# First MoE chunk: weights asked for in pairs; wide copies of probabilities moved to VectorE in the sink-free groups

## The chip, the cores and the metric

The kernel runs on one core of one Trainium2 chip. The metric is the device time of one execution in microseconds (us), median of several runs. The engines are TensorE (PE; its weight loads are PEld), VectorE (DVE), ScalarE (ACT), GpSimd (POOL) and SyncE (SP), which issues most DMAs. Each engine takes its own instructions in the order of the program and waits where one isn't ready.

## The reference

Attention with sink keys and a sliding window, then two feed-forward layers:

```python
# attention: q, k, v are 2 x 8 heads x 768 x 64, n_sink = 4, window = 128
scores = scale * q @ k.T
keep = is_sink | in_window
scores = np.where(keep, scores, -1000000000.0)
a = np.exp(scores - max); a = a / (sum(a) + 1e-09)
x = (a @ v)                      # as 1536 tokens x 512
# MoE 1: 512 -> 1536 -> 512
g = x @ w_gate; silu = g * (1.0 / (1.0 + np.exp(-g)))
x = silu * (x @ w_val) @ w_out
# MoE 2: 512 -> 2048 -> 512
h = x @ w_in
g = np.maximum(h, 0.0) + alpha * np.minimum(h, 0.0)
out = g @ w_out
```

The expert weights arrive as 64-bit floats (the kernel reads them as pairs of 32-bit words) and are split on the chip.

## The kernel before, in words

**Attention.** Tokens are handled in 24 groups: two heads (one head pair, `hp`) by two query blocks of 128. The first eight, numbered 0 to 7 here in program order, begin at query block 0 of a sequence (`i0 == 0`) and are sink-free: their keys are only blocks 0 and 1. `attention()` runs a software pipeline over groups: scores of group x, values of group x-2, flips of group x-1, `norm` of x, `prep` of x+2.

- `prep` transposes k and q on PE and copies them out on ACT (`th`).
- `scores` (L265) makes two score tiles for each of the two query blocks t = 0, 1. DVE adds the mask and takes a row maximum (L271; in later groups after a predicated copy, L269); ACT takes the exponential and its row sum (L275, `pr`).
- `norm` makes reciprocals of the sums on DVE (L291, L292, `rinv`); POOL multiplies the probabilities by them (L298 in sink-free groups, L307 and L308 in others).
- `flip` transposes probabilities on PE (L320, `ps_p` in PSUM) and copies them to SBUF as `pt`. In sink-free groups ACT does this (L324), 256 columns wide for t = 0 and 512 for t = 1. In the others DVE multiplies by a triangle mask on the way (L326, 512 wide).
- `values` multiplies by v on PE (L351, `xp`); ACT rounds the result to `xh` (L847), DVE makes the rest `xl` (L848).

**Weights.** `Stream` loads weight tiles of 128x512 in the order of `seq` (SP), and `convert` turns each into a rounded part `wh` and a rest `wl`: ACT (L587), DVE TENSOR_SCALAR (L589), DVE SCALAR_TENSOR_TENSOR twice (L592, L595), ACT `wh` (L604), DVE `wl` (L605). One tile is converted at each call of `tick`, into one of 12 slots; seven more slots are added when attention is over. `done` gives slots back. `moe1_seq` writes the order of the first layer: chunks of four gate tiles (`wg`), four value tiles (`wv`), four output tiles (`wo`).

**MoE.** `Moe1.unit(c, b)` handles chunk c of the hidden features for 512 tokens (pass b): for each pair of features two gate products `pg`, then two value products `pv`, each 12 matmuls (L656 to L658: `wh` by `xh`, `wh` by `xl`, `wl` by `xh`, for four slices kk of the 512 inputs, one for each head pair), then the output product `po`. Pass 0 needs `xh` and `xl` of groups 0 to 7; slice kk needs the two groups of head pair kk, the last of them groups 4 to 7. Units (0, 0) and (0, 1) are woven between attention groups 8 to 23; the last pass of chunk 0 and all else run after attention.

The order on each engine is decided by the framework's scheduler when the program is built; an edit at one place can so move instructions of others.

Of the kernel before, what the change touches and what calls it, by code (L numbers as in the profile page):

```python
# [11 lines left out]
AF = mybir.ActivationFunctionType  # L12
# [11 lines left out]
NF1 = FF1 // P  # L24
# [9 lines left out]
CHUNK = 4  # L34
# [10 lines left out]
DOWN = float(2.0**-112)  # L45
# [94 lines left out]
class Group:  # L140
# [169 lines left out]
    def flip(self, t):  # L310
        nc, g = self.nc, self.g
        w, blk, sp, kk = self.blocks(t)
        if t == 0:
            self.pt = g.pt_p.tile([P, 2, 2 * NG, P], F32, tag="pt", name="pt")
        nb = len(blk)
        ps = g.ps_t.tile([P, 512], F32, tag="ps", name="ps_p")
        for e in range(2):
            for x, c in enumerate(blk):
                y = (e * nb + x) * P
                nc.tensor.transpose(ps[:, y:y + P], self.pr(t, e, c, P), g.ident)  # L320
        b0 = max(0, 2 * t - self.off)
        psv = ps[:, :2 * nb * P].rearrange("p (e c) -> p e c", e=2)
        if sp is None:
            nc.scalar.activation(self.pt[:, :, b0:b0 + nb].rearrange("p e a c -> p e (a c)"), psv, AF.Copy)  # L324
        else:
            nc.vector.tensor_tensor(  # L326
                out=self.pt[:, :, b0:b0 + 2], in0=psv.unsqueeze(2).to_broadcast([P, 2, 2, P]),
                in1=g.tri.unsqueeze(1).to_broadcast([P, 2, 2, P]), op=ALU.mult,
            )
        if t == NG - 1 and self.sink:  # L330
            self.pts = g.pt_p.tile([P, P], F32, tag="pts", name="pts")
            ps = g.ps_t.tile([P, 512], F32, tag="ps", name="ps_p2")
            nc.tensor.transpose(ps[:, 0:P], self.sk.rearrange("p x s -> p (x s)"), g.ident)
            nc.scalar.activation(self.pts, ps[:, 0:P], AF.Copy)
# [203 lines left out]
def new_acc(g, name):  # L538
    for pool in g.acc_ps:
        if pool[1]:  # L540
            pool[1] -= 1
            return pool[0].tile([P, KD, T], F32, tag="acc", name=name), pool
    assert False


def big(g, dt, name):
    return g.x_p.tile([P, KD, T], dt, tag="x", name=name)
# [83 lines left out]
def moe1_seq(wg, wv, wo):  # L631
    seq = []
    for c in range(NF1 // CHUNK):
        fs = range(c * CHUNK, (c + 1) * CHUNK)
        step = CHUNK if c == 0 else 2
        for f in fs[::step]:
            seq += [(0, wg, x, DOWN, x) for x in range(f, f + step)]
            seq += [(0, wv, x, DOWN, NF1 + x) for x in range(f, f + step)]
        seq += [(1, wo, f, DOWN, 2 * NF1 + f) for f in fs]
    return seq  # L640

# [10 lines left out]
def proj(nc, ps, w, xh, xl):  # L652
    wh, wl = w
    for kk in range(KD):
        c = slice(kk * P, (kk + 1) * P)
        nc.tensor.matmul(ps, wh[:, c], xh[:, kk], start=(kk == 0), stop=False)  # L656
        nc.tensor.matmul(ps, wh[:, c], xl[:, kk], start=False, stop=False)  # L657
        nc.tensor.matmul(ps, wl[:, c], xh[:, kk], start=False, stop=(kk == KD - 1))  # L658
# [5 lines left out]
def hidden_pair(g):  # L664
    return [g.h_p.tile([P, 2, T], F32R, tag=t, name=t) for t in ("hh", "hl")]


def split_hidden(nc, hid, hh, hl):
    nc.scalar.activation(hh, hid, AF.Copy)  # L669
    nc.vector.tensor_tensor(out=hl, in0=hid, in1=hh, op=ALU.subtract)  # L670


class Moe1:
# [4 lines left out]
    def unit(self, c, b):  # L678
        nc, g, st = self.nc, self.g, self.st
        nch = NF1 // CHUNK  # L680
        w0 = self.base + c * 3 * CHUNK

        def at(kind, x):
            return w0 + (kind * CHUNK + x if c == 0 else 2 * (x - x % 2) + 2 * kind + x % 2)

        xh, xl = self.xs[b]
        last = b == len(self.xs) - 1
        hid_of = []
        for x in range(0, CHUNK, 2):
            pair = hidden_pair(g)  # L690
            pss, sgs = [], []
            for r in range(2):
                ps = g.ps_m.tile([P, 512], F32, tag="ps", name="pg")
                proj(nc, ps, st.get(at(0, x + r)), xh, xl)
                pss.append(ps)
                if r == 0:
                    yield
            for ps in pss:
                sg = g.t_p.tile([P, T], F32, tag="sg", name="sg")
                nc.scalar.activation(sg, ps, AF.Silu)  # L700
                sgs.append(sg)
            yield
            for r in range(2):
                hh, hl = (t[:, r] for t in pair)
                ps = g.ps_m.tile([P, 512], F32, tag="ps", name="pv")
                proj(nc, ps, st.get(at(1, x + r)), xh, xl)
                hid = g.t_p.tile([P, T], F32, tag="hid", name="hid")
                nc.vector.tensor_tensor(out=hid, in0=ps, in1=sgs[r], op=ALU.mult)  # L708
                split_hidden(nc, hid, hh, hl)
                hid_of.append((hh, hl))  # L710
                if last and r == 1 and (c or x + 2 == CHUNK):
                    st.done(4 if c else 2 * CHUNK)
                yield
        if c == 0:
            self.accs[b] = new_acc(g, "acc1")
        acc, home = self.accs[b]
        if c == nch - 1:
            yh, yl = big(g, F32R, "yh"), big(g, F32R, "yl")
        for m in range(KD):
            mc = slice(m * P, (m + 1) * P)  # L720
            ps = g.ps_m.tile([P, 512], F32, tag="ps", name="po")
            for x, (hh, hl) in enumerate(hid_of):
                wh, wl = st.get(w0 + 2 * CHUNK + x)
                nc.tensor.matmul(ps, wh[:, mc], hh, start=(x == 0), stop=False)  # L724
                nc.tensor.matmul(ps, wl[:, mc], hh, start=False, stop=False)  # L725
                nc.tensor.matmul(ps, wh[:, mc], hl, start=False, stop=(x == CHUNK - 1))  # L726
            av = acc[:, m]
            if c == 0:
                nc.scalar.activation(av, ps, AF.Copy)
            else:  # L730
                nc.vector.tensor_tensor(out=av, in0=ps, in1=av, op=ALU.add)
            if c == nch - 1:
                split_hidden(nc, av, yh[:, m], yl[:, m])
            yield
        if c == nch - 1:
            home[1] += 1
            self.put(yh, yl)
        if last:
            st.done(CHUNK)
# [78 lines left out]
def fast(nc, tc, ctx, g, n_sink, window, alpha, q, k, v, w_gate, w_val, w_out, x2_in, x2_out, out):  # L818
    g.x_p = ctx.enter_context(tc.tile_pool(name="x_p", bufs=2 * NPASS))
    weight_pools(nc, tc, ctx, g, "")  # L820
    add_pool(nc, tc, ctx, g.acc_ps, "acc_p", NPASS - 1)
    st = Stream(nc, g, moe1_seq(w_gate, w_val, w_out) + moe2_seq(g, x2_in, x2_out))
    xs = [(big(g, F32R, "xh"), big(g, F32R, "xl")) for _ in range(NPASS)]
    m1, m2 = moe(nc, g, st, xs, out, [[blk * NG * P for blk in pair] for pair in ORDER])
# [63 lines left out]
def general(nc, tc, g, q, k, v, w_gate, w_val, w_out, x2_in, x2_out, out):  # L888
    g.exact = True
    with ExitStack() as ctx:  # L890
        xp = ctx.enter_context(tc.tile_pool(name="gx", bufs=1))
        xh = xp.tile([P, KD, NT], F32R, name="gxh")
        xl = xp.tile([P, KD, NT], F32R, name="gxl")
        for b in range(B):
            g.xh, g.xl = xh[:, :, b * S:(b + 1) * S], xl[:, :, b * S:(b + 1) * S]
            dense(nc, tc, g, q, k, v, b)
        g.x_p = ctx.enter_context(tc.tile_pool(name="gy", bufs=2))
        weight_pools(nc, tc, ctx, g, "_g")
        add_pool(nc, tc, ctx, g.acc_ps, "acc_g", 2)
        g.w2_p = ctx.enter_context(tc.tile_pool(name="w2_g", bufs=1))  # L900
        for p in range(NPASS):
            xs = [tuple(t[:, :, p * T:(p + 1) * T] for t in (xh, xl))]
            st = Stream(nc, g, moe1_seq(w_gate, w_val, w_out) + moe2_seq(g, x2_in, x2_out))
            mix(nc, g, st, *moe(nc, g, st, xs, out, [[p * T]]))
# [40 lines left out]
```

## Time and profile before

| | us |
|---|---|
| median of 3 runs | 692.17 |
| lowest and highest | 690.24, 692.19 |
| profiled execution, its own time | 691.42 |
| its span from first to last instruction | 689.6 |

The span is what the trace covers; 1.8 us of the profiled execution lie outside it. Mean granted TensorE clock over the span: 0.989 of full speed. PE is busy for 96% of the span, DVE for 59%, ACT for 43%, POOL for 7%.

### The profile page before, as it was taken

The numbers are of one execution on the slowest core, as the hardware profiler recorded it, in microseconds if no ns is written. First come the engines' busy times: TensorE is split into PE (matmuls) and PEld (weight loads), VectorE is DVE, ScalarE is ACT, GpSimd is POOL, SyncE is SP. The second block draws the span as 40 slices with busy tenths as digits, with TensorE's granted clock in tenths as the row PEclk, the third lists the DMA queues.
The fourth block names the chain that finished last, engine by engine and source line by source line (L and its number), as shares of the span: only waits on it lengthen the run. The fifth ranks groups of instructions, "written<-read, shape, count | busy, mean of one in ns | idle before, by whom it ended". The sixth has DMA issues, their size and how long they took to land.

```text
span 689.6 us, 8978 instructions
## 1 busy us (share of the span) xinstructions
PE 664.4 (96%) x3195; PEld 530.1 (77%) x3195; DVE 406.8 (59%) x925; ACT 297.9 (43%) x684; POOL 47.2 (7%) x82
## 2 busy tenths in 40 slices
PE   5789999999999999999999999999999999999996
PEld 3556777677678888888888888888888888888885
DVE  5899538656379962379642599427933844333432
ACT  4887546555366722054422365436612532113320
POOL 2433013311100000000000000000000000000000
PEclk9879999999999999999999999999999999999999
DMA  9875414421025630033400043301510000000111
GB/s 164 203 215 167 119 26 109 94 58 23 12 82 181 192 126 0 1 103 118 148 0 1 0 153 118 97 1 61 154 31 0 1 0 1 1 0 1 61 62 66
DMA packets 76276, 50.87 MB, mean 74 GB/s; under 512 B 50624, under 2 KB 71104, under 8 KB 76224
## 3 DMA queue, kind: packets, MB, share of 16 engines
q1 hardware_dynamic: 73872, 50.22, 25.6%
q8 instruction: 27, 0.44, 0.3%
q10 hardware_dynamic: 2352, 0.01, 0.2%
q14 instruction: 25, 0.20, 0.1%
HBM read 47.07 MB, written 3.15 MB: 73 GB/s over the span
## 4 chain that ended last, share of the span: by engine, by line
PE 88%; DVE 4%; ACT 3%; DMA 2%; POOL 1%; issue 1%; SPq 0%; DVEq 0%; ACTq 0%; POOLq 0%
PE ph L658 6%; PE ph L656 6%; PE pf L782 6%; PE pf L780 6%; PE pf L781 6%; PE ph L657 6%; PE po L724 5%; PE pv L656 5%; PE po L726 5%; PE pg L656 5%; PE pv L658 5%; PE po L725 5%; PE pv L657 5%; PE pg L657 5%; PE pg L658 5%; PE ps_s L265 2%
## 5 line engine op out<-in xcount | busy, mean ns | idle before, releaser
L669 ACT ACTIVATE hh<-hid 128x512 fp32r<-128x512 f32 x84 | 52.9, 630 | 78.4 <-DVE hid L708 47.4
L670 DVE TENSOR_TENSOR hl<-hid,hh 128x512 fp32r<-128x512 f32 x84 | 58.1, 692 | 31.5 <-ACT hh L669 31.4
L656 PE MATMUL ph<-yh,wh 128*128 128x512 f32 x192 | 74.8, 390 | 0.0
L762 ACT ACTIVATE neg<-ph,sal 128x512 f32<-128x512 f32 x48 | 33.0, 687 | 96.8 <-PE ph L658 96.6
L658 PE MATMUL ph<-yh,wl 128*128 128x512 f32 x192 | 74.7, 389 | 0.0
L657 PE MATMUL ph<-yl,wh 128*128 128x512 f32 x192 | 74.7, 389 | 0.0
L780 PE MATMUL pf<-wh,hh 128*128 128x512 f32 x192 | 74.7, 389 | 0.0
L781 PE MATMUL pf<-wl,hh 128*128 128x512 f32 x192 | 74.7, 389 | 0.0
L782 PE MATMUL pf<-wh,hl 128*128 128x512 f32 x192 | 72.4, 389 | 0.0
L604 ACT ACTIVATE wh<-w_m 128x512 fp32r<-128x512 f32 x68 | 42.9, 635 | 51.9 <-DVE w_m L595 18.6
L605 DVE TENSOR_TENSOR wl<-w_m,wh 128x512 fp32r<-128x512 f32 x68 | 47.7, 706 | 23.1 <-ACT wh L604 22.5
L764 DVE SCALAR_TENSOR_TENSOR hid<-ph,sig,neg 128x512 f32<-128x512 f32 x48 | 36.0, 750 | 39.6 <-ACT neg L762 39.4
L656 PE MATMUL pg<-xh,wh 128*128 128x512 f32 x144 | 57.0, 397 | 0.0
L724 PE MATMUL po<-hh,wh 128*128 128x512 f32 x144 | 56.7, 395 | 0.0
L656 PE MATMUL pv<-xh,wh 128*128 128x512 f32 x144 | 56.7, 393 | 0.0
L657 PE MATMUL pg<-xl,wh 128*128 128x512 f32 x144 | 56.3, 391 | 0.0
L658 PE MATMUL pg<-xh,wl 128*128 128x512 f32 x144 | 56.1, 390 | 0.0
L658 PE MATMUL pv<-xh,wl 128*128 128x512 f32 x144 | 56.1, 390 | 0.0
L725 PE MATMUL po<-hh,wl 128*128 128x512 f32 x144 | 56.1, 390 | 0.0
L657 PE MATMUL pv<-xl,wh 128*128 128x512 f32 x144 | 56.1, 389 | 0.0
L787 DVE TENSOR_TENSOR acc<-pf,acc 128x512 f32<-128x512 f32 x36 | 23.2, 686 | 50.5 <-PE pf L782 50.5
L726 PE MATMUL po<-hl,wh 128*128 128x512 f32 x144 | 52.7, 390 | 0.0
(122 smaller groups left out, 1211.2 us busy)
## 6 DMA issues: line engine op xcount, KB each, us to landing
w_raw<-in_moe_w_out SPq DMA_DIRECT2D x28, 512.0 KB, 3.4
w_raw<-in_moe_w_in SPq DMA_DIRECT2D x16, 512.0 KB, 3.8
w_raw<-in_moe_w_gate SPq DMA_DIRECT2D x12, 512.0 KB, 3.6
w_raw<-in_moe_w_val SPq DMA_DIRECT2D x12, 512.0 KB, 3.9
vr<-in_v SPq DMA_DIRECT2D x32, 96.0 KB, 2.9
out<-acc SPq DMA_DIRECT2D x12, 256.0 KB, 2.2
qr<-in_q SPq DMA_DIRECT2D x32, 64.0 KB, 2.1
kr<-in_k SPq DMA_DIRECT2D x16, 96.0 KB, 2.2
```

Of the source, the lines that this page charges most:

```text
L605: nc.vector.tensor_tensor(out=wl, in0=w32, in1=wh, op=ALU.subtract)
L656: nc.tensor.matmul(ps, wh[:, c], xh[:, kk], start=(kk == 0), stop=False)
L657: nc.tensor.matmul(ps, wh[:, c], xl[:, kk], start=False, stop=False)
L658: nc.tensor.matmul(ps, wl[:, c], xh[:, kk], start=False, stop=(kk == KD - 1))
L669: nc.scalar.activation(hh, hid, AF.Copy)
L670: nc.vector.tensor_tensor(out=hl, in0=hid, in1=hh, op=ALU.subtract)
L724: nc.tensor.matmul(ps, wh[:, mc], hh, start=(x == 0), stop=False)
L725: nc.tensor.matmul(ps, wl[:, mc], hh, start=False, stop=False)
L726: nc.tensor.matmul(ps, wh[:, mc], hl, start=False, stop=(x == CHUNK - 1))
L780: nc.tensor.matmul(ps, hh[:, ts], wh, start=(x == 0), stop=False)
L781: nc.tensor.matmul(ps, hh[:, ts], wl, start=False, stop=False)
L782: nc.tensor.matmul(ps, hl[:, ts], wh, start=False, stop=(x == CHUNK - 1))
```

## The change: order of the first chunk's weights, and the engine of eight copies

Two edits, which don't touch the same lines.

First, `moe1_seq` asked for chunk 0 as four gate tiles, then four value tiles; now it asks, as for the other chunks, for two gates, two values, two gates, two values. `at` finds the tiles by the new places. In the last pass `done` gives back four slots after each pair of features, where it gave back all eight after the second pair.

Second, in `flip` of the sink-free groups the copy for t = 1 (512 columns) is made by DVE and no more by ACT. These are eight copies; those for t = 0 (256 columns) stay on ACT.

```diff
@@ flip
         if sp is None:
-            nc.scalar.activation(self.pt[:, :, b0:b0 + nb].rearrange("p e a c -> p e (a c)"), psv, AF.Copy)
+            dst = self.pt[:, :, b0:b0 + nb].rearrange("p e a c -> p e (a c)")
+            if t:
+                nc.vector.tensor_copy(dst, psv)
+            else:
+                nc.scalar.activation(dst, psv, AF.Copy)
         else:
@@ moe1_seq
-        step = CHUNK if c == 0 else 2
-        for f in fs[::step]:
-            seq += [(0, wg, x, DOWN, x) for x in range(f, f + step)]
-            seq += [(0, wv, x, DOWN, NF1 + x) for x in range(f, f + step)]
+        for f in fs[::2]:
+            seq += [(0, wg, x, DOWN, x) for x in range(f, f + 2)]
+            seq += [(0, wv, x, DOWN, NF1 + x) for x in range(f, f + 2)]
         seq += [(1, wo, f, DOWN, 2 * NF1 + f) for f in fs]
@@ Moe1.unit
         def at(kind, x):
-            return w0 + (kind * CHUNK + x if c == 0 else 2 * (x - x % 2) + 2 * kind + x % 2)
+            return w0 + 2 * (x - x % 2) + 2 * kind + x % 2
...
-                if last and r == 1 and (c or x + 2 == CHUNK):
-                    st.done(4 if c else 2 * CHUNK)
+                if last and r == 1:
+                    st.done(4)
```

In the changed kernel the lines behind `flip` have higher numbers: L589, L592, L595, L605 are L593, L596, L599, L609; L656 to L658 are L659 to L661; L848 is L851.

How the order on the engines changes, at three places. The first is DVE's queue between the reciprocals of group 4 and the first score tiles of group 5 (`ps_s` with `mask_68`). Before:

```order
L292 RECIPROCAL rinv<-rinv 128x4
L589 TENSOR_SCALAR w_m<-w_m 128x512
L592 SCALAR_TENSOR_TENSOR w_m<-w_raw,w_m 128x512
L271 ISA ps_s,nb<-ps_s,mask_68 128x128
L271 ISA nb 128x1
L595 SCALAR_TENSOR_TENSOR w_m<-w_raw,w_m 128x512
```

The same place in the changed kernel:

```order
L596 SCALAR_TENSOR_TENSOR w_m<-w_raw,w_m 128x512
L292 RECIPROCAL rinv<-rinv 128x4
L599 SCALAR_TENSOR_TENSOR w_m<-w_raw,w_m 128x512
L326 COPY pt<-ps_p 128x2x256
L609 TENSOR_TENSOR wl<-w_m,wh 128x512
L271 ISA ps_s,nb<-ps_s,mask_68 128x128
```

A copy of probabilities now stands ahead of the scores, and the last two steps of a weight conversion (L599, L609) have moved from behind the first score tile to ahead of it.

The second is DVE's queue at `xl` of group 6. Before:

```order
L605 TENSOR_TENSOR wl<-w_m,wh 128x512
L595 SCALAR_TENSOR_TENSOR w_m<-w_raw,w_m 128x512
L269 COPY_PREDICATED ps_s<-above,ps_s 128x128
L271 ISA ps_s,nb<-ps_s,mask_a 128x160
L271 ISA nb 128x1
L271 ISA ps_s,nb<-ps_s,mask_b 128x160
L271 ISA nb 128x1
L848 TENSOR_TENSOR xl<-xp,xh 128x256
```

In the changed kernel:

```order
L609 TENSOR_TENSOR wl<-w_m,wh 128x512
L596 SCALAR_TENSOR_TENSOR w_m<-w_raw,w_m 128x512
L269 COPY_PREDICATED ps_s<-above,ps_s 128x128
L271 ISA ps_s,nb<-ps_s,mask_b 128x160
L271 ISA nb 128x1
L599 SCALAR_TENSOR_TENSOR w_m<-w_raw,w_m 128x512
L593 TENSOR_SCALAR w_m<-w_m 128x512
L271 ISA ps_s,nb<-ps_s,mask_b 128x160
L271 ISA nb 128x1
L851 TENSOR_TENSOR xl<-xp,xh 128x256
L326 COPY pt<-ps_p 128x2x256
```

The eighth copy comes right behind `xl` of group 6, and more of the weight conversions stands ahead of it. Counted from the start of DVE's queue to this `xl`, the changed kernel has seven copies, two TENSOR_SCALAR (11 for 9), one L596 (10 for 9), one L599 (10 for 9), one L609 (9 for 8) and one mask reduction (36 for 35) more.

The third is PE's queue at the first gate product, with tile numbers (`pg_738` is the first product, `pg_777` the second; `ps_p` and `ps_p2` are flips of group 8). Before, the end of the first product and the start of the second:

```order
L656 MATMUL pg_738<-xh_90,wh_318 128x512
L657 MATMUL pg_738<-xl_91,wh_318 128x512
L658 MATMUL pg_738<-xh_90,wl_319 128x512
L320 MATMUL ps_p_765<-ident_61,pr_642 128x128 x2
L320 MATMUL ps_p_769<-ident_61,pr_642 128x128 x2
L333 MATMUL ps_p2_774<-ident_61,sk_684 128x128
L656 MATMUL pg_777<-xh_90,wh_383 128x512
```

In the changed kernel, the end of the second product:

```order
L661 MATMUL pg_777<-xh_90,wl_384 128x512
L659 MATMUL pg_777<-xh_90,wh_383 128x512
L660 MATMUL pg_738<-xl_91,wh_318 128x512
L661 MATMUL pg_738<-xh_90,wl_319 128x512
L660 MATMUL pg_777<-xl_91,wh_383 128x512
L661 MATMUL pg_777<-xh_90,wl_384 128x512
```

The last two matmuls of the first product (slice kk = 3, which needs `xl` of group 7) now come behind ten of the second. All that PE has ahead of them is in the order of before.

## Rows read from the trace of the kernel before

**Rows 1.** Page: busy us and share of the span by engine.
```profile
PE 664.4 (96%) x3195; PEld 530.1 (77%) x3195; DVE 406.8 (59%) x925; ACT 297.9 (43%) x684; POOL 47.2 (7%) x82
```

**Rows 2.** Busy us by stretch; the header names the columns, (x) are instructions.
```profile
core 0: us, PE busy (x) PEld busy (x) DVE busy (x) ACT busy (x) POOL busy (x), PEclk, DMA share, GB/s
...
14.50:30.00 15.50, 12.11 (x81) 8.03 (x80) 12.88 (x45) 14.67 (x52) 5.29 (x7) 0.96 0.90 203
30.00:41.60 11.60, 9.89 (x58) 6.48 (x57) 9.59 (x24) 7.75 (x23) 6.02 (x7) 0.76 0.75 204
41.60:59.20 17.60, 14.21 (x76) 8.60 (x75) 17.00 (x56) 15.08 (x52) 5.67 (x10) 0.81 0.77 217
...
190.00:690.00 500.00, 492.40 (x2184) 407.24 (x2182) 280.04 (x467) 185.46 (x332) 0.00 (x0) 1.00 0.19 61
```

**Rows 3.** Waits of PE from 60 us to the end: total us, times, longest.
```profile
PE xp L351 <- DVE pt L326: 2.0, 3, 1.1
PE xp L351 <- ACT pts L334: 1.1, 1, 1.1
```

**Rows 4.** Timeline of PE: start, us, instruction, merged neighbours (x), idle before.
```profile
48.94 1.11 PE L320 MATMUL ps_p<-ident,pr 128*128 128x128 f32 x4 [0.49 <-POOL pr L298]
...
58.37 0.87 PE L351 MATMUL xp<-pt,vr 128*64 128x256 f32 x8
59.17 0.50 PE L656 MATMUL pg<-xh,wh 128*128 128x512 f32 x1
...
66.23 0.39 PE L656 MATMUL pv<-xh,wh 128*128 128x512 f32 x1
```

**Rows 5.** Waits of DVE from 14.5 to 59.2 us.
```profile
DVE ps_s L271 <- PE ps_s L265: 2.4, 2, 1.4
DVE w_m L589 <- ACT w_m L587: 1.1, 2, 0.7
DVE ps_s L269 <- PE ps_s L265: 0.5, 1, 0.5
DVE xl L848 <- ACT xh L847: 0.5, 1, 0.5
DVE wl L605 <- ACT wh L604: 0.5, 1, 0.5
```

**Rows 6.** Timeline of DVE, 30 to 65 us.
```profile
33.87 0.30 DVE L271 CUSTOM_DVE_ANT_0 ps_s<-ps_s,mask 128x128 f32<-128x128 f32 x1 [1.43 <-PE ps_s L265]
...
41.05 0.69 DVE L605 TENSOR_TENSOR wl<-w_m,wh 128x512 fp32r<-128x512 f32 x1
...
56.21 0.41 DVE L848 TENSOR_TENSOR xl<-xp,xh 128x256 fp32r<-128x256 f32 x1
56.54 0.32 DVE L271 CUSTOM_DVE_ANT_0 ps_s<-ps_s,mask_b 128x160 f32<-128x160 f32 x1
...
63.80 1.28 DVE L326 TENSOR_TENSOR pt<-ps_p,tri 128x512 f32<-128x512 f32 x2
64.99 0.68 DVE L595 SCALAR_TENSOR_TENSOR w_m<-w_raw,w_m 128x512 uint32<-128x512 uint32 x1
```

**Rows 7.** Groups by form on ACT, 14.5 to 59.2 us: count, busy us, mean ns.
```profile
L324 ACT ACTIVATE pt<-ps_p 128x512 f32<-128x512 f32 x8 | 4.9, 614 | 1.3 <-PE ps_p L320 1.3
```

**Rows 8.** Timeline of DVE after attention.
```profile
208.87 0.69 DVE L592 SCALAR_TENSOR_TENSOR w_m<-w_raw,w_m 128x512 int32<-128x512 int32 x1
209.47 0.42 DVE L589 TENSOR_SCALAR w_m<-w_m 128x512 int32<-128x512 int32 x1
209.81 0.69 DVE L595 SCALAR_TENSOR_TENSOR w_m<-w_raw,w_m 128x512 uint32<-128x512 uint32 x1
```

**Rows 9.** Groups by form, 14.5 to 59.2 us, on DVE and on POOL.
```profile
L592 DVE SCALAR_TENSOR_TENSOR w_m<-w_raw,w_m 128x512 int32<-128x512 int32 x10 | 9.6, 957 | 0.1
...
L298 POOL TENSOR_TENSOR pr<-pr,rinv 128x512 f32<-128x512 f32 x8 | 10.0, 1252 | 0.0
L298 POOL TENSOR_TENSOR pr<-pr,rinv 128x256 f32<-128x256 f32 x7 | 4.3, 613 | 18.2 <-DVE rinv L292 13.8 <-ACT pt L324 3.9 <-ACT th L232 0.5
```

## The prediction

> **What bounds the kernel now.** I began with the busy shares: PE is busy for 664.4 of 689.6 us [rows 1], so PE's queue is the kernel, and the question is where PE still waits. The table by stretch [rows 2] says when: from 190 us on, PE is busy for 492.40 of 500 us, but between 14.5 and 59.2 us only for 12.11 of 15.50, 9.89 of 11.60 and 14.21 of 17.60. PE's waits behind 60 us come to 3.1 us in four pieces, all on `pt` or `pts` of late attention groups [rows 3]. So the time is the moment of the first gate product, 59.17 us [rows 4], plus 630 us in which PE hardly stops. What comes earlier or later there comes out at the end, and little behind it can win a delay back.
>
> What sets 59.17? In 14.5 to 30 us ACT is the fullest (14.67 of 15.50, DVE 12.88); from 30 us it is DVE, and in the last stretch DVE has 17.00 of 17.60 against ACT's 15.08 [rows 2]. DVE idles for 2.62 + 2.01 + 0.60 = 5.2 us in all three. Of these it waits 2.9 us for score tiles of PE (1.4 us at one place, 33.87 us [rows 6]) and 2.1 us for ACT [rows 5].
>
> **The pairs.** They matter only if somebody waits for a value weight. In the old order the first value tile is the fifth converted; its last step ends at 41.05 + 0.69 = 41.74 us [rows 6], and the first value product is at 66.23 us [rows 4]. It lies ready for 24 us, so bringing it forward is worth 0. Two loads of equal size change places: 0. The earlier `done` lets conversions use old slots earlier in the last pass; that lies behind 190 us, where DVE has 280.04 of 500 us of work and PE never waits for a weight [rows 2, 3]. The cover is PE's own queue; without it, PE would wait for one conversion, some 0.34 + 3 x 0.60 = 2.1 us of DVE [rows 8].
>
> **The copies.** ACT loses eight, 4.9 us busy [rows 7]. DVE gains eight. The trace has no DVE copy out of PSUM, so the price is bounded: not below the TENSOR_SCALAR of one 128x512 operand, 0.34 us from start to start (209.47 to 209.81 [rows 8]); not above the two-input operation where POOL gets in its way, 0.96 us [rows 9]. Nearest is L326: it reads the same PSUM tile and writes the same `pt`, with one input more. Two take 63.80 to 64.99 us, 0.60 each [rows 6]. I take that: 8 x 0.60 = 4.8 us, bounds 2.7 and 7.7.
>
> [...]
>
> **What moves with them.** Ahead of `xl` of group 6 DVE now has two TENSOR_SCALAR, three 0.60 us steps of conversions and a mask reduction more (counts at the second place in the order): 2 x 0.34 + 3 x 0.60 + 0.33 (56.21 to 56.54) = 2.8 us [rows 6, 8]. That work isn't new, it is done earlier than it need be. It counts in full because the eighth copy stands behind it, and `values` of group 7, which PE runs just ahead of the first gate product, reads that copy.
>
> **The sum.** `xl` of group 6 ended at 56.21 + 0.41 = 56.62 us [rows 6]. The eighth copy ends 4.8 + 2.8 = 7.6 us later, at 64.2, if DVE keeps its idle time, and at 64.2 - 5.2 = 59.0 if it loses all of it. `values` of group 7 ran at 58.37 [rows 4]. So PE is late by 0.6 to 5.8 us. How much idle goes? At the 1.43 us wait the new order puts a copy and two conversion steps, 1.8 us, ahead of the score tile: that wait is gone. The 2.1 us on ACT should mostly go, since ACT has 4.9 us less to do. Of the remaining 1.7 us I let half go. That is 1.4 + 2.1 + 0.9 = 4.4 us, so the copy ends at 59.8 and PE is late by 1.4 us.
>
> Do the copies wait themselves? What stands behind one on DVE is `xl` and the reciprocals, on which POOL waits, and on POOL the flips: PE's wait for `pr` at 48.94 us is of this kind. That flip, of group 6, is over at 48.94 + 1.11 = 50.05 [rows 4], more than 6 us before `xl` of group 6 starts at 56.21 [rows 6], and its copy stands in between with room on both sides; I charge no wait. Where a flip comes late after all, DVE's idle time is kept, which is the upper end above. The two moved PE matmuls give `xl` of group 7 ten matmuls of time, so I charge nothing for it; without them its 0.4 us and the steps ahead of it would be PE's wait.
>
> The profiled execution took 691.42 us; 1.4 more is 692.8. The median of the runs shown is 692.17, 0.75 above it, and would give 693.6, the lowest run 690.24 would give 691.6. I say **693.0 us**. A measurement of this kernel can tell about 0.3%, 2.1 us, from no change.
>
> **Rivals.**
>
> *The copies vanish in DVE's gaps (no effect, within 0.6 us).* For it: 0.6 us is the sum with all idle absorbed, and at the low price of a copy the sum falls by 2.1 us and DVE is no longer what PE waits for. Against it: DVE has only 0.60 us free from 41.6 to 59.2 us, where the last copies fall. 691.4 to 692.2.
>
> *Slower: DVE stays as idle as it was.* The place is DVE's queue ahead of the eighth copy, the price 5.8 us, or 697.2; it passes 2.1 us if less than 3.7 of the 5.2 us idle are absorbed (5.8 - 2.1). For it: DVE works in order, and each copy adds a wait for PE's flips to a queue in which scores and sums already wait. Against it: the places above, where queued work fills the gaps.
>
> *Faster: the stalls of DVE go.* L592 takes 957 ns here and 690 after attention, so ten of them lose 2.7 us [rows 8, 9]; POOL multiplies for 14.3 us in that stretch [rows 9]. If copies rather than conversions ran beside POOL, this could come back: the copy would end at 59.0 - 2.7 = 56.3 with no idle left, and PE could go up to 2.1 us ahead of before, 689.3. [...] Against it: it needs no idle and no stall on DVE at once. [...]
>
> *The pairs do something.* Only if PE waited for a weight, which it doesn't; 2.1 us either way.
>
> **How the numbers follow.** Forecast, 0.6 to 2.1 us late: 0.43. No effect: 0.17. Slower rival, over 2.1 us: 0.30. Faster rival: 0.08. Pairs: 0.02. By over 0.3% faster are 0.07 of the faster rival (the rest stops short of 2.1 us) and half of the pairs, 0.08; slower are 0.30 and the other half of the pairs, 0.31; within are 0.43, 0.17 and the 0.01 left, 0.61. The range takes in half of the faster rival and most of the slower one: 690.5 to 696.3. The forecast's own range is 692.0 to 694.2.
>
> **What would show it.** Right: the eight copies at about 0.6 us each; DVE busy for 17 us or more of the last 17.6 ahead of the first gate product, with a gap total well below 5.2 us; the first gate product at 60 to 61 us; behind it the same 630 us. Wrong: copies near 0.35 or 0.95 us; a first gate product ahead of 59 us, with L592 near 690 ns or PE's clock at full level from 30 to 59 us (faster rival); DVE idle for 3 us or more and a start behind 61.3 us (slower rival); or a first gate product where I expect it and a new wait of PE behind 60 us, which would break the step that nothing changes there.

## The result and the profile after

| | before | after |
|---|---|---|
| median, us (5 runs each) | 692.17 | 695.26 |
| lowest and highest | 690.24, 692.40 | 694.64, 695.87 |
| profiled execution, us | 691.42 | 694.64 |
| its span, us | 689.6 | 692.9 |

After over before is 1.0054, with a 95% interval of 1.0042 to 1.0067: slower by over 0.3%. (The two medians alone, of five runs each, give 1.0045.) The time lies in the range and 2.3 us above the number forecast; it is outside the forecast's own range, 692.0 to 694.2, and in that of the slower rival.

The busy time by stretch answers to [rows 2]:

```profile
14.50:30.00 15.50, 10.61 (x79) 7.21 (x79) 14.70 (x48) 13.01 (x47) 4.68 (x6) 1.00 0.97 218
30.00:41.60 11.60, 9.33 (x51) 6.44 (x53) 10.81 (x26) 6.90 (x23) 4.54 (x6) 0.71 0.71 194
41.60:59.20 17.60, 12.32 (x70) 7.74 (x66) 17.41 (x50) 12.70 (x42) 6.47 (x10) 0.81 0.68 194
59.20:62.50 3.30, 2.42 (x16) 1.35 (x16) 3.30 (x11) 2.61 (x10) 0.58 (x2) 1.00 0.42 120
```

The third busy column is DVE. Up to 59.2 us it idles for 0.80 + 0.79 + 0.19 = 1.8 us; before it was 5.2. PE, the first, has less done in each of the first three stretches. Its clock is not what changed: granted in these three were 0.96, 0.76 and 0.81 before [rows 2], now 1.00, 0.71 and 0.81. PE's timeline, against [rows 4]:

```profile
50.43 0.44 PE L320 MATMUL ps_p<-ident,pr 128*128 128x128 f32 x2 [1.80 <-POOL pr L298]
51.88 1.12 PE L320 MATMUL ps_p<-ident,pr 128*128 128x128 f32 x4 [1.01 <-POOL pr L298]
...
60.09 1.72 PE L265 MATMUL ps_s<-th 64*128 64x288 f32 x8 [0.93 <-ACT pr L275]
61.73 0.87 PE L355 MATMUL xp<-pt,vr 128*64 128x256 f32 x8
62.53 0.50 PE L659 MATMUL pg<-xh,wh 128*128 128x512 f32 x1
```

The first gate product is at 62.53, 3.36 us later than before. From there to the end are 692.9 - 62.53 = 630.4 us, as before (689.6 - 59.17 = 630.4). So the whole loss lies ahead of 62.53 us. The flip of group 6 (51.88) was at 48.94 before: 2.94 of the 3.36 us are lost by then.

PE's waits for POOL's product, first after (30 to 62.5 us), then before (30 to 59.2 us):

```profile
PE ps_p L320 <- POOL pr L298: 6.9, 5, 2.7
```

```profile
PE ps_p L320 <- POOL pr L298: 1.2, 2, 0.8
```

What made POOL late is seen in DVE's timeline at group 6. After:

```profile
46.25 0.67 DVE L596 SCALAR_TENSOR_TENSOR w_m<-w_raw,w_m 128x512 int32<-128x512 int32 x1
...
47.06 0.16 DVE L291 TENSOR_SCALAR rinv<-ssum 128x4 f32<-128x4 f32 x1
...
47.85 0.71 DVE L599 SCALAR_TENSOR_TENSOR w_m<-w_raw,w_m 128x512 uint32<-128x512 uint32 x1
48.48 0.41 DVE L593 TENSOR_SCALAR w_m<-w_m 128x512 int32<-128x512 int32 x1
...
49.16 0.17 DVE L292 RECIPROCAL rinv<-rinv 128x4 f32<-128x4 f32 x1
```

Before:

```profile
46.09 0.16 DVE L291 TENSOR_SCALAR rinv<-ssum 128x4 f32<-128x4 f32 x1
...
46.75 0.17 DVE L292 RECIPROCAL rinv<-rinv 128x4 f32<-128x4 f32 x1
```

The sum's small first step (L291) is 0.97 us later, and the reciprocal (L292) 2.41 later: two conversion steps, 48.81 - 47.85 = 0.96 us, and a mask reduction now stand between the two. DVE has no gap there; what is late is a short step, because longer ones stand ahead of it in the queue. POOL's product of this group, after, then before:

```profile
49.47 2.35 POOL L298 TENSOR_TENSOR pr<-pr,rinv 128x256 f32<-128x256 f32 x2 [1.45 <-DVE rinv L292]
```

```profile
47.10 1.79 POOL L298 TENSOR_TENSOR pr<-pr,rinv 128x256 f32<-128x256 f32 x2 [0.51 <-ACT th L232]
```

It starts 2.37 us later and takes 0.56 us longer; together that is the delay of the flip.

### The profile page after: what moved, and what is told of

Read it like the earlier page. It is cut to its first block, busy times and chain, and to the rows that moved or that the text cites. A ratio compares the mean times of both kernels' runs of the same rounds, so it can differ in the third digit from the quotient of the medians.

```text
span 692.9 us, 8985 instructions
## 1 busy us (share of the span) xinstructions
PE 662.9 (96%) x3195; PEld 529.6 (76%) x3195; DVE 411.7 (59%) x933; ACT 294.4 (42%) x676; POOL 46.9 (7%) x82
## 4 chain that ended last, share of the span: by engine, by line
PE 87%; DVE 6%; DMA 2%; SPq 2%; ACT 1%; issue 1%; POOL 0%; DVEq 0%; ACTq 0%; POOLq 0%
PE ph L659 6%; PE ph L660 6%; PE pf L783 6%; PE pf L784 6%; PE pf L785 6%; PE ph L661 6%; PE po L727 5%; PE pg L659 5%; PE po L729 5%; PE pv L659 5%; PE po L728 5%; PE pv L660 5%; PE pv L661 5%; PE pg L660 5%; PE pg L661 5%; PE xp L355 2%
## 5 line engine op out<-in xcount | busy, mean ns | idle before, releaser
L659 PE MATMUL ph<-yh,wh 128*128 128x512 f32 x192 | 74.8, 389 | 0.0
L661 PE MATMUL ph<-yh,wl 128*128 128x512 f32 x192 | 74.7, 389 | 0.0
L609 DVE TENSOR_TENSOR wl<-w_m,wh 128x512 fp32r<-128x512 f32 x68 | 49.9, 737 | 23.7 <-ACT wh L608 23.5
L659 PE MATMUL pg<-xh,wh 128*128 128x512 f32 x144 | 57.1, 397 | 0.3 <-ACT pr L275 0.2
L659 PE MATMUL pv<-xh,wh 128*128 128x512 f32 x144 | 56.6, 393 | 0.0
L661 PE MATMUL pg<-xh,wl 128*128 128x512 f32 x144 | 56.1, 390 | 0.0
L661 PE MATMUL pv<-xh,wl 128*128 128x512 f32 x144 | 56.1, 390 | 0.0
```

The lines of the kernel that those rows point to most:

```text
L609: nc.vector.tensor_tensor(out=wl, in0=w32, in1=wh, op=ALU.subtract)
```

## The experiments

Two theories. **Count** is that of the prediction: PE waits for the end of DVE's work up to the eighth copy, so each us of work ahead of it that no idle time absorbs is a us lost. **Loop**: groups follow one another through scores (PE), mask (DVE), exponential (ACT), reciprocal (DVE), product (POOL), flip (PE) and copy; what counts is which DVE steps stand inside one turn of this loop, not their sum. In the table stand, from the traces, the moment at which POOL begins its product for groups 5, 6 and 7, the first gate product, and what is left of the span behind it ("rest"):

| kernel | group 5 | group 6 | group 7 | first gate product | rest | ratio |
|---|---|---|---|---|---|---|
| before | 38.52 | 47.10 | 51.53 | 59.17 | 630.4 | 1 |
| after | 40.63 | 49.47 | 53.03 | 62.53 | 630.4 | 1.0054 |
| copies alone | 40.75 | 49.59 | 53.16 | 62.50 | 630.5 | 1.0053 |
| pairs alone | 39.22 | 47.79 | 52.22 | 59.89 | 630.4 | 0.9996 |
| copies of groups 0 to 3 | 40.76 | 47.99 | 51.39 | 59.48 | 631.0 | 1.0015 |
| copies of groups 4 to 7 | 38.67 | 49.12 | 52.68 | 60.43 | 630.3 | 1.0027 |
| all 16 copies on DVE | 41.77 | 48.31 | 53.44 | 63.31 | 629.2 | 1.0054 |
| after, 4 held | 41.96 | 50.65 | 54.01 | 64.19 | 630.0 | 1.0059 |
| after, 8 held | 40.61 | 44.08 | 47.55 | 53.20 | 635.2 | 0.9968 |
| old order, copies on ACT, 6 held | 38.59 | 45.90 | 49.49 | 55.72 | 632.3 | 0.9988 |
| pairs, copies on ACT, 6 held | 39.30 | 47.23 | 50.04 | 56.03 | 632.6 | 0.9980 |
| pairs, copies on ACT, 8 held | 38.55 | 42.32 | 45.62 | 50.98 | 633.5 | 0.9933 |
| the same, held to group 7 | 38.45 | 42.23 | 45.52 | 50.89 | 631.8 | 0.9894 |
| pairs, copies on ACT, 10 held | 34.05 | 37.18 | 40.48 | 47.56 | 636.7 | 0.9923 |

"Held" are the last of the first 12 weight conversions, whose steps on DVE were put behind `xl` of group 6 by an order between instructions alone (8 held: conversions 5 to 12). Ratios are to the kernel before, timed on the same chip.

**Each part alone.** The copies on DVE with the old order of weights:

```diff
-            nc.scalar.activation(self.pt[:, :, b0:b0 + nb].rearrange("p e a c -> p e (a c)"), psv, AF.Copy)
+            dst = self.pt[:, :, b0:b0 + nb].rearrange("p e a c -> p e (a c)")
+            if t:
+                nc.vector.tensor_copy(dst, psv)
+            else:
+                nc.scalar.activation(dst, psv, AF.Copy)
```

> The eight wide copies on DVE, the weights asked for in the old order. Theory (the copies lengthen DVE's queue ahead of the first gate product, the pairs do nothing): all of the loss, ratio 1.0045 +- 0.001, 695.3 us, first gate product near 62.5 us as in the changed kernel (before: 59.17). Rival (the loss comes from the pairs, which move loads and slots): ratio 1.000 to 1.002, first gate product below 61 us.

And the change with that piece taken back, so the pairs alone.

> The weights in pairs, all copies on ACT. Theory: no effect, ratio 1.000 +- 0.001, first gate product at 59.2 +- 0.4 us. Rival (the pairs cost or give something): a first gate product moved by over 0.6 us, or new waits of PE behind 60 us, ratio at least 0.0015 from 1.

The copies alone: 695.50 us, ratio 1.0053 (1.0039 to 1.0066), first gate product at 62.50. The pairs alone: 691.71, 0.9996 (0.9987 to 1.0005). The copies are the whole loss, and the pairs are worth nothing. (The first gate product of the pairs alone came at 59.89, 0.72 later than before, which was a sign of the rival; but its profiled execution took 0.64 us longer too, and the medians differ by 0.13 us. So one profile can be off by as much.)

**Half of the copies.** Old order of weights; the eight groups are numbered, and the condition in `flip` is `t and self.n < 4` in one kernel, `t and self.n >= 4` in the other.

> Old order of weights; only groups 0 to 3 copy on DVE. Theory 1 (what counts is how much of DVE's idle time is left where the copy falls: 2.6 + 2.0 us free up to 41.6 us): nearly free, +0 to +0.8 us, ratio 1.000 to 1.0012. Theory 2 (each copy costs alike, and what it pushes): half of the loss, +1.7 us, ratio 1.0024. Theory 3 (relief of ACT, which was fullest from 14.5 to 30 us, pays): -0.5 to -1.5 us.

> Old order of weights; only groups 4 to 7 copy on DVE. Theory 1 (DVE has only 0.6 us free from 41.6 to 59.2 us): +1.8 to +3 us, ratio 1.0026 to 1.0043, more than the first four. Theory 2 (each copy costs alike): +1.7 us, the same as the first four. In both, DVE is busy for over 17.2 us of the last 17.6 ahead of the first gate product.

The first four: 692.29, 1.0015 (1.0005 to 1.0024). The last four: 693.93, 1.0027 (1.0017 to 1.0037). Together 0.42% of 0.53%: both halves cost something, by the medians the last four more, as Theory 1 has it; the intervals overlap, so equal shares are not excluded, and they leave open whether the halves add up. The table shows where. With the first four alone, group 5 is 2.24 us late and the first gate product only 0.31: a delay can be made up when no copies follow. With the last four alone, group 5 is on time and group 6 2.02 us late, and two conversion steps and a mask reduction stand between its L291 and L292 as in the change (the profiled execution, 692.48 us, is one of the fastest of its nine).

**All sixteen copies**, those for t = 0 too; old order of weights.

```diff
-            if t:
-                nc.vector.tensor_copy(dst, psv)
-            else:
-                nc.scalar.activation(dst, psv, AF.Copy)
+            nc.vector.tensor_copy(dst, psv)
```

> Old order of weights; both copies of each sink-free group on DVE, eight of 512 and eight of 256 columns. Theory (length of DVE's queue): 8 more operations, 0.33 us each as xl of 256 columns has it, 2.6 us, and with no idle time left to take them the loss grows from 3.4 to 5.5 to 7 us, ratio 1.008 to 1.010. Rival (only the wide copies hurt, by a wait of their own): no more than with eight, ratio 1.005.

694.70, 1.0054 (1.0040 to 1.0067): eight copies more cost nothing. Count's forecast missed here. The scheduler put fewer conversion steps ahead of `xl` of group 6 this time (one TENSOR_SCALAR and one SCALAR_TENSOR_TENSOR fewer, as many `wl` as after), which takes back only some 0.9 us of the eight copies' price. But DVE's queue did not get longer: up to the end of the eighth wide copy DVE was busy for 45.8 us (after: 45.2) and idle for 0.8 (1.8), so that this copy was over at 61.09, 0.4 us earlier than after:

```profile
60.48 0.68 DVE L326 COPY pt<-ps_p 128x512 f32<-128x512 f32 x1
61.09 0.41 DVE L593 TENSOR_SCALAR w_m<-w_m 128x512 int32<-128x512 int32 x1
```

And PE did not wait for it. From 57.80 us to the first gate product PE had no gap; from 59.2 to 62.5 us its granted clock was 0.50, where after had 1.00:

```profile
59.22 2.75 PE L265 MATMUL ps_s<-th 64*128 64x288 f32 x8
61.90 1.47 PE L355 MATMUL xp<-pt,vr 128*64 128x256 f32 x8
```

**Conversions held back.** The first kernel is the change with 8 held:

```diff
     def convert(self):
-        nc, g, i = self.nc, self.g, self.n_conv
+        g, i = self.g, self.n_conv
+        if 4 <= i < 3 * CHUNK and not g.exact and g.hold is not None:
+            with g.tc.issue_after(g.hold):
+                self.steps()
+        else:
+            self.steps()
...
-                nc.vector.tensor_tensor(out=xl[:, hp, ts], in0=src, in1=xh[:, hp, ts], op=ALU.subtract)
+                rest = nc.vector.tensor_tensor(out=xl[:, hp, ts], in0=src, in1=xh[:, hp, ts], op=ALU.subtract)
+                if n == 0 and half == 1 and hp == 2:
+                    g.hold = rest.ins
```

> The changed kernel, with the DVE steps of weight conversions 5 to 12 held behind xl of group 6 on DVE's queue (an edge of order alone). Ahead of that xl DVE then has four conversions instead of nine, some 5 x 2.1 = 11 us less. Theory (the start of the gate products is set by the length of DVE's queue, of which the copies are 4.8 us and conversions over 20): the first gate product comes ahead of 59.2 us, at 54 to 58, and the time is below before, ratio 0.992 to 0.999, unless held conversions make PE wait behind it. Rival (the copies cost through waits: flips, copy, values, whatever else DVE has to do): still 1.5 us or more behind before, ratio over 1.002.

The second has the pairs and the same hold, with the copies on ACT.

> Pairs, copies on ACT, conversions 5 to 12 held in the same way. Theory: first gate product at 53 to 57 us, ratio 0.990 to 0.998; against the kernel with copies on DVE and the same hold the difference is under 1.5 us, since DVE now has room for them. Rival (copies cost by waits): the difference between the two is 3 us or more, as without the hold. If conversions come too late, PE waits on wl or wh at the products of the second pair of features.

The third is the kernel before with 6 held (`6 <= i` in place of `4 <= i`).

> The kernel before (four gates, then four values, copies on ACT) with conversions 7 to 12 held behind xl of group 6: the first products need the first, second, fifth and sixth, so two more must stay ahead than with pairs. Theory: six conversions instead of eight ahead of that xl, 4 to 5 us less on DVE, first gate product at 56 to 58 us, ratio 0.995 to 0.999, between before and the pairs with the hold. Rival (DVE's queue does not set the start): first gate product at 59.2 +- 0.5, ratio 1.000.

688.76, ratio 0.9968 (0.9956 to 0.9981); 686.36, 0.9933 (0.9919 to 0.9946); 690.26, 0.9988 (0.9979 to 0.9997). By the ratios the first is 0.86% of the kernel before, some 5.9 us, faster than the change although it makes the same copies. Count had forecast all three ratios rightly (the first gate products, 53.20, 50.98 and 55.72, came even earlier than its ranges), so they don't speak against it; the difference of the first two, 2.4 us, lies between what it said (under 1.5) and what the rival said (3 or more). What these runs add is a loop without conversions in it. A turn of the first one's, in DVE's timeline (its profiled execution took 690.23 us, 1.5 more than its median):

```profile
43.52 0.17 DVE L291 TENSOR_SCALAR rinv<-ssum 128x4 f32<-128x4 f32 x1 [0.91 <-ACT pr L275]
43.73 0.18 DVE L292 RECIPROCAL rinv<-rinv 128x4 f32<-128x4 f32 x1
43.82 0.66 DVE L326 COPY pt<-ps_p 128x512 f32<-128x512 f32 x1
44.40 0.41 DVE L859 TENSOR_TENSOR xl<-xp,xh 128x256 fp32r<-128x256 f32 x1
44.73 0.29 DVE L271 CUSTOM_DVE_ANT_0 ps_s<-ps_s,mask 128x128 f32<-128x128 f32 x1
...
46.99 0.17 DVE L291 TENSOR_SCALAR rinv<-ssum 128x4 f32<-128x4 f32 x1 [0.90 <-ACT pr L275]
```

With no conversion in between, a turn takes 46.99 - 43.52 = 3.47 us; in the change groups 5 and 6 are 49.47 - 40.63 = 8.84 us apart on POOL, before 47.10 - 38.52 = 8.58. Not every turn with conversions is so long (groups 6 and 7: 3.56 after, 4.43 before). Over the three turns from group 4 to group 7, POOL takes 20.14 us after the change, 20.25 before, and 13.86 here. So it is the conversions' steps, there before the change too, that stretch the loop.

The copy, 0.58 of the 3.47 us, stands in the turn as well (next step at 44.40), between the reciprocals and the next group's mask. But it does not lengthen it: with the copies on ACT the turns of groups 5 to 7 take 3.77 and 3.30 us, and from POOL's start on group 5 to the first gate product it is 12.43 us against 12.59. Of the 2.22 us between the two first gate products 2.06 are there at group 5 already (40.61 and 38.55), where conversions still stand in the turns; some 0.8 of these may be that one execution's (it has group 1 at 18.11, the changed kernel in the same order at 17.31). So in these two profiles a copy on DVE costs next to nothing where the conversions are gone. Where all of the 2.4 us between the medians comes from is not settled, the less so as the granted clock differs too: 0.71 from 30 to 41.6 us, with copies on ACT 0.85. The kernel with copies on ACT shows the other side in its busy times (compare the second and third line of after):

```profile
30.00:41.60 11.60, 9.74 (x62) 6.85 (x63) 7.38 (x26) 8.93 (x31) 5.56 (x8) 0.85 0.76 198
41.60:59.20 17.60, 17.38 (x109) 12.83 (x108) 14.44 (x56) 15.22 (x50) 7.65 (x12) 1.00 0.54 135
```

PE is busy for 17.38 of 17.60 us at a granted 1.00, where after had 12.32 at 0.81.

**The change with 4 held** (`8 <= i`): about 4.0 us of DVE steps fewer ahead of `xl` of group 6.

> The changed kernel, but the DVE steps of conversions 9 to 12 stand behind `xl` of group 6. Ahead of that `xl` DVE has three TENSOR_SCALAR, four SCALAR_TENSOR_TENSOR and one `wl` step fewer than in the changed kernel, about 3 x 0.34 + 5 x 0.60 = 4.0 us. Theory (these steps count in full, since DVE is busy almost throughout): 695.3 - 4.0 = 691.3, ratio 0.997 to 1.001, the first gate product at 58 to 59.5 us. Rival (the copies cost by what stands behind them, the score-to-reciprocal loop, and the steps only fill what would be idle): within 1.2 us of the changed kernel, ratio 1.003 to 1.006, first gate product behind 61.3 us.

695.96, 1.0059 (1.0046 to 1.0072): no gain. Count wanted 691. Its busy times, rows of DVE's timeline, and PE's values of group 7:

```profile
14.50:30.00 15.50, 12.38 (x79) 8.30 (x78) 12.89 (x42) 12.18 (x42) 4.00 (x5) 1.00 0.96 215
30.00:41.60 11.60, 8.86 (x45) 5.84 (x45) 10.79 (x29) 8.07 (x28) 3.99 (x4) 0.71 0.62 176
41.60:59.20 17.60, 11.69 (x64) 7.45 (x65) 16.59 (x50) 12.17 (x42) 7.49 (x11) 0.81 0.66 184
```

```profile
21.77 0.69 DVE L326 COPY pt<-ps_p 128x512 f32<-128x512 f32 x1 [1.62 <-PE ps_p L320]
...
60.18 1.78 DVE L601 TENSOR_SCALAR w_m<-w_m 128x512 int32<-128x512 int32 x2
61.88 0.77 DVE L604 SCALAR_TENSOR_TENSOR w_m<-w_raw,w_m 128x512 int32<-128x512 int32 x1
62.57 0.68 DVE L326 COPY pt<-ps_p 128x512 f32<-128x512 f32 x1
```

```profile
63.40 0.87 PE L355 MATMUL xp<-pt,vr 128*64 128x256 f32 x8 [1.97 <-DVE pt L326]
```

DVE idles for 2.61 + 0.81 + 1.01 = 4.4 us, 2.6 more than after: most of the work taken out came back as idle time, and `xl` of group 6 begins at 59.87, only 0.7 us earlier than after (60.56). One gap is a copy that waits for its flip, with the reciprocals of group 2 behind it; POOL begins that group at 23.55, in after at 22.08. This lag of 1.5 us is not the edit's: DVE's steps and PE's matmuls have the order of the changed kernel up to there and far beyond (the ninth conversion begins on DVE at 52.36 in after).

Nor does the run decide between the theories. Three held steps came out between `xl` and the eighth copy, and PE waited 1.97 us for that copy. Without this wait the first gate product would have been at about 64.19 - 1.97 = 62.2, an estimate, against 62.53 in after. Here the end of DVE's work up to the eighth copy is the bound, as Count has it; the edit took 3.7 us of work from ahead of `xl` and put part of it where it did harm.

**The order of the weights again, and how far holding goes.** Pairs, copies on ACT: with 6 held (to compare with the old order with 6 held), with 10 held (`2 <= i`), and with 8 held behind `xl` of group 7 (`hp == 3`).

> Pairs, all copies on ACT, the DVE steps of conversions 7 to 12 behind `xl` of group 6. It differs from the run in the old order with the same six held back in the order of the weights alone; the counts of steps ahead of `xl` are the same in both. Theory (the order of the weights is worth nothing, only the number of steps ahead counts): ratio 0.998 to 1.0, first gate product at 55.2 to 56.2 us. Rival (with conversions held back the pairs begin to matter, because a value weight becomes late in the old order): ratio at or below 0.996 with the same first gate product, and the old order showing a wait of a value product that this one does not show.

> Pairs, all copies on ACT, the DVE steps of conversions 3 to 12 behind `xl` of group 6: only the first two gates are converted ahead of it, two conversions or 4.2 us of DVE less than with four. Theory (with four PE was already its own bound up to 51 us, and the value weights now come late): no better than with four, ratio 0.993 to 0.997, a wait of a value product for a weight step, and the first gate product not ahead of 50.0 us. Rival (DVE's work ahead of it is still the price): ratio 0.988 to 0.991, first gate product at 47 to 49 us.

> Pairs, all copies on ACT, conversions 5 to 12 behind `xl` of group 7 (in the run with 4 held ahead they stand behind `xl` of group 6): two TENSOR_SCALAR and four SCALAR_TENSOR_TENSOR, 3.1 us, leave the stretch between the two. Theory (PE is its own bound there): within 1.2 us of that run, ratio 0.9925 to 0.996. Rival (`xl` of group 7 still comes late behind those steps): 1.5 to 3 us better, ratio 0.989 to 0.9912.

Six held, in pairs: 690.29, 0.9980 (0.9971 to 0.9989). The old order gave 690.26 and 0.9988, and the intervals overlap, so no worth of the order shows here either. Ten held: 686.07, 0.9923 (0.9910 to 0.9937). The first gate product came at 47.6 us, 3.4 earlier than with eight, which the theory put out of reach; the time is the same all the same, since the rest of the span is 3.2 us longer. From 62.5 to 95 us the granted clock is lower, 0.95 against 1.00, and output products wait for late weights (with eight held they wait too, 2.2 us, but for other operands):

```profile
PE po L731 <- ACT wh L612: 2.1, 2, 1.7
```

Eight held to group 7: **684.21, 0.9894 (0.9879 to 0.9908)**, the fastest, 7.35 us below the kernel before (691.56 on the same chip). Each against its own chip's kernel before (the one behind group 6 was 4.75 us below), it is 2.6 us better than behind group 6, the rival's size, but not by the rival's way: the first gate product stays at 50.9. PE is busier by 0.22 and 0.67 us in these stretches, of 1.8 us by which the spans differ. Over the whole span PE's busy time is 1.0 us shorter (659.9 against 660.9, for as many matmuls); why, I did not find.

```profile
41.60:59.20 17.60, 17.60 (x111) 13.23 (x110) 13.86 (x53) 13.36 (x45) 7.38 (x13) 1.00 0.43 107
...
62.50:95.00 32.50, 30.92 (x161) 22.83 (x160) 25.87 (x65) 24.55 (x54) 5.64 (x6) 1.00 0.51 149
```

The kernel with eight held behind group 6 has 17.38 us of PE in the first of them (its row stands further up), and in the last:

```profile
62.50:95.00 32.50, 30.25 (x144) 22.02 (x142) 24.78 (x62) 23.22 (x50) 4.77 (x5) 1.00 0.52 154
```

## Why the prediction was right and where not

**Right: what sets the end.** In the change the time moved with the first gate product, and the 630 us behind it stayed; the only new wait of PE behind it is 0.2 us of a gate product on an exponential. The step has a limit that the held kernels show: where the first gate product comes much earlier, the rest grows. With 8 held and the copies on DVE it came 5.97 us ahead of before and the rest was 4.8 us longer, 2.2 of them waits of output products. From 62.5 to 95 us its granted clock was 0.95, before 1.00; what that cost was not measured apart.

**Right: the pairs,** of which neither comparison shows an effect.

**Right: the price of a copy.** 0.60 us from start to start, the value taken from L326. The group by form and the eighth copy in DVE's timeline, after:

```profile
L326 DVE COPY pt<-ps_p 128x512 f32<-128x512 f32 x8 | 5.4, 675 | 0.2 <-PE ps_p L320 0.2
```

```profile
60.56 0.41 DVE L851 TENSOR_TENSOR xl<-xp,xh 128x256 fp32r<-128x256 f32 x1
60.90 0.68 DVE L326 COPY pt<-ps_p 128x512 f32<-128x512 f32 x1
61.49 0.68 DVE L596 SCALAR_TENSOR_TENSOR w_m<-w_raw,w_m 128x512 int32<-128x512 int32 x1
```

**Off: the sum, in two terms.** The eighth copy ended at 61.49, not at 59.8. From 14.5 us to there DVE was busy for 47.0 - 1.8 = 45.2 us; before, to the end of `xl` of group 6, for 42.1 - 5.2 = 36.9. The work grew by 8.3 us where the sum had 4.8 + 2.8 = 7.6, and of the idle time 3.4 us were absorbed where I took 4.4. That is 4.9 us net in place of 3.2: 0.7 and 1.0 of the 1.7 missing. Both errors went the same way. By the prediction's own terms the slower rival's condition, under 3.7 us absorbed, came true, and one of its signs, a start behind 61.3 us, but not the other (DVE idle for 3 us or more). The range held because it took in most of that rival; the forecast, late by 0.6 to 2.1 us, did not come true with 3.36.

**Wrong: "I charge no wait" for what stands behind a copy.** The prediction named the path (reciprocals, POOL, flips) and gave it 6 us of room because the flip of group 6 was over long before `xl` of group 6. That room was measured at one place of a loop in which a group's delay can be handed on to the next. POOL's start of groups 4 to 7, before and after: 31.28 and 32.89, 38.52 and 40.63, 47.10 and 49.47, 51.53 and 53.03. Late by 1.6 already at group 4, and by 2.4 at group 6. POOL makes up 0.9 us at group 7, but PE, with the flip of group 6 late in its queue, does not: its flips of group 7 begin at 56.33, before at 53.70.

The sum took the end of DVE's queue as the bound. In the change PE did not wait for it: PE's last wait ahead of the first gate product is 0.93 us for an exponential, at 60.09, and the values of group 7 follow at 61.73 without a gap, when the eighth copy is over (61.49). That the two came out within some 0.2 us of each other is luck, and so is how near the sum came. Which of the two comes last differs from kernel to kernel: with all 16 copies on DVE it was not the copy, with 4 held it was, by 1.97 us. So the queue's end is one bound and the loop another, and the prediction left out the second.

**The faster rival's first half holds, for copies.** A copy beside POOL wasn't stalled, the conversion step behind it was. The eighth product of POOL, and DVE beside it, after:

```profile
53.03 1.61 POOL L298 TENSOR_TENSOR pr<-pr,rinv 128x256 f32<-128x256 f32 x2 [1.21 <-ACT wh L608]
```

```profile
53.03 0.69 DVE L326 COPY pt<-ps_p 128x512 f32<-128x512 f32 x1 [0.17 <-PE ps_p L320]
53.64 1.55 DVE L596 SCALAR_TENSOR_TENSOR w_m<-w_raw,w_m 128x512 int32<-128x512 int32 x1
```

The copy takes 0.69; the step that follows takes 1.55 where its clean time is 0.69 [rows 8], and POOL is done at 54.64. The copy at 33.28, beside POOL as well, takes 0.68, and so do those without POOL beside them, as at 20.11 and 60.90. Why the copy keeps its time there and the step behind it does not, no run shows. The copies beside POOL brought nothing back, since the stalls moved to other steps: from 14.5 to 62.5 us L596 takes 770 ns on average (957 before, as L592 [rows 9]), but L609 954 (787 before, as L605).

**Open.** No kernel put back only the two conversion steps that now stand between L291 and L292 of group 6, so their share of the loss is read from the trace and not measured. Nor is it settled how the copies' cost divides between their own time and the steps that the scheduler moved with them. That the copies are the whole loss is measured; that they cost it by way of the loop is read from the traces.

## What to carry to other kernels

When groups run through a loop over several engines, ask of each long step on an in-order engine which short step stands behind it and who waits for that; adding up busy time against idle time gives the end of that engine's queue, and who waits for it has to be read. Work that nobody needs yet (here weight conversions, ready up to 24 us early) was not free in the gaps of the engine that carries the loop: with the copies on ACT, holding eight conversions back took the ratio from 0.9996 to 0.9933. Hold it back until the loop is through, but not past the moment its first user comes (with ten held, output products waited 2.1 us for weights). Before a copy is moved from one engine to another, look at what stands behind it in the loop, and not only at which engine is fuller. And a start that comes earlier by several us need not come out at the end: here 6 us gained at the first gate product were some 2.4 us of time.

## What was not expected of the hardware

PE's granted clock was not the same in all kernels: 0.71 and 0.81 of full speed from 30 to 41.6 and from 41.6 to 59.2 us after the change, 0.85 and 1.00 with eight conversions held back and the copies on ACT, where PE is busy for 17.38 of the last 17.60 us. So a part of what the hold won may be PE's work done at a higher granted clock; how much was not measured apart, and what sets the clock no run shows.
